# First batch's packed values times w_in: pieces three to eight as three bursts of 512 columns instead of six of 256

## The chip, the cores and the metric

The kernel runs on one core of one Trainium2 chip. The metric is the device time of one execution in microseconds (us); the median of three runs of the kernel before is 786.12 us (785.88 to 786.27). The engines are named as in the profile: PE (TensorE) with its weight loads (PEld), DVE (VectorE), ACT (ScalarE), POOL (GpSimd) and SP (SyncE, which issues the DMAs here).

## The reference

Two attentions, each over 8 batches and 8 heads of width 64, then a feed-forward layer with a rational activation:

```
p_packed = sm_attn(p, k, v)              # 32 packed queries against 576 keys
out      = sm_attn(q, p_packed, p_packed)  # 576 queries against 32 packed keys
x  = out as (4608, 512)
h  = x @ w_in                            # 512 -> 2048
P  = a0 + a1*h + a2*h^2 + a3*h^3
Q  = 1 + |b0|*|h| + |b1|*h^2
out = (P / (Q + 1e-6)) @ w_out           # 2048 -> 512
```

All of it in float32; w_in and w_out arrive as float64 and are taken as their 64-bit words.

## The kernel before, in words

For each batch the kernel never forms `x`. It multiplies the packed values by w_in first (`m`, called M in the code: 2 groups of 128 rows, 2048 columns) and then the softmax weights of the second attention (`AH`) by that: h = m times AH. The 2048 columns of w_in are eight pieces of 256 (`NCH` = 8, `CF` = 256); `m_chunk(bb, c, n)` at lines 786 to 809 makes n of them for batch `bb`, from piece c on. One call is a burst of eight PE products of 64x32 weights into two PSUM tiles of the ring `at` (two buffers of 512 float32 columns), one for each head group, and then, for the first batch, one ACT copy from each PSUM tile into `m`; later batches split into a high and a low part. The ring `at` also serves the attention of all later batches, and the remainder rows.

The feed-forward work is 128 units (batch, half of the 576 rows, piece c). `hidden` (line 814) is one: two tiles `h`, and for each three ACT passes (`Y`, `U`, `sq`) and two DVE passes (`Y` times h, then the step with `abS`), one POOL addition (`U` plus `sq`), two ACT passes (`V`), and two or three DVE passes that end in `gh` or `gl`, the left operand of the last product. `acc_block` (line 893) multiplies it by w_out, three units later, into `acc`. The first 12 units are not divided into a high and a low part; there `gh` belongs to even and `gl` to odd pieces. In the answers of the trace and in the orders below a name such as `h_17` is the 17th tile of that ring: `h_1` and `h_2` are unit 0, `h_17` and `h_18` unit 8; `gh_1`, `gl_1`, `gh_2`, ... are units 0, 1, 2, ...

The float64 words of w_in and w_out come in sixteen pieces, taken into float32 by `convert` (line 429): two ACT passes and three DVE passes (one of them the group that the profile calls CUSTOM_DVE_ANT_0 and the order ISA). In the order below `w_6`, `w_4`, `w_8` are the raw words of w_in's pieces 5, 6 and 7 (counted from one), `w_7`, `w_5`, `w_12`, `w_13` those of w_out.

The text of the kernel does not set the order of issue. Every operation is recorded (all of them appear as line 226 in the profile, the zero products below as line 223) and `Planner` (lines 32 to 231) orders them by a list schedule: costs per engine from a table, priority by the longest way to the end, four rounds, first in, first out on each engine. A buffer ring's turns follow the recorded order, so what is recorded when does matter. The loop at lines 966 to 985 records two halves of each unit u; at each half step `filler(i)` records the burst that `mt` names for step i, and those of the 16 stages of the next batch's attention that `fill` puts there. These stages are spread over the steps of a range that `mt` does not use (line 951). Where the planner's own schedule leaves PE idle early on, `idle` (line 992) adds products with a zero operand into an open accumulation, which change no value.

Of the kernel before, what the change touches and what calls it, by code (L numbers as in the profile page):

```python
# [257 lines left out]
def attention_rational_ffn(  # L258
# [23 lines left out]
    NCH = DF // CF  # L282
# [655 lines left out]

    STEPS = 16
    mt, fill, rem = {}, {}, {}  # L940
    for c in range(1, NCH):
        mt[max(0, 2 * c - 3)] = 0, c
    for bb in range(1, B):
        for c in range(0, NCH, 2):
            mt[2 * UB * bb + 2 * c - 7] = bb, c, 2
# [95 lines left out]
```

## Time and profile before

| | before |
|---|---|
| median of three runs | 786.12 us |
| profiled execution, its time | 788.12 us |
| profiled execution, its span | 786.0 us |
| PE busy | 745.8 us (95%) |
| DVE busy | 693.2 us (88%) |
| ACT busy | 657.8 us (84%) |
| POOL busy | 453.6 us (58%) |
| TensorE clock granted, mean | 0.987 |

A stage table gives the busy time of each engine in a stretch of the span; a chain of waits gives the work that ended last, step by step, with what released it; a row of the timeline gives start, duration, engine and operation, and in brackets the idle time before it and what ended that. Names are out<-in by the program's names, without buffer numbers. The busy time of PE is partly modelled: a row of products that waits inside its run shows as longer.

### The profile page before, as it was taken

The page shows a single profiled execution, that of the slowest core. Times are in us where ns is not written, and L with a number is a line of the kernel's source. Part 1 is how long each engine was busy: PE and PEld are TensorE (multiplying, and loading weights), DVE is VectorE, ACT ScalarE, POOL GpSimd, SP SyncE. Part 2 cuts the span into 40 slices and gives each one's busy share as a digit, 9 for nine tenths or more (in the row PEclk, how much of TensorE's full clock was granted, in tenths as well). Part 3 has the DMA queues.
Part 4 walks back from the last instruction along what each step waited for, and adds up shares of the span by engine and source line. Part 5 has one row for each costly group of instructions (what it writes and reads, how often), then busy time and mean ns, then how long its engine had stood idle before and what let it go on. Part 6 is the DMA issues. An engine that isn't in the chain of part 4 may idle for free.

```text
span 786.0 us, 14945 instructions
## 1 busy us (share of the span) xinstructions
PE 745.8 (95%) x5336; PEld 567.5 (72%) x5336; DVE 693.2 (88%) x1295; ACT 657.8 (84%) x1464; POOL 453.6 (58%) x448
## 2 busy tenths in 40 slices
PE   2679999999999999999999999999999999999997
PEld 1345555588778887678778887678787887778886
DVE  4899999998999789998999789998999789988873
ACT  5869978988896998888897898889798788998872
POOL 0012448757585665756686555756587556766663
PEclk9959999999999999999999999999999999999999
DMA  9984353023601155023601136023701132000001
GB/s 297 332 296 143 108 100 49 1 85 46 110 1 55 45 66 90 1 85 46 95 17 55 44 52 104 1 58 62 94 28 54 41 45 46 1 22 7 27 1 41
DMA packets 152027, 56.03 MB, mean 71 GB/s; under 512 B 122256, under 2 KB 141200, under 8 KB 151952
## 3 DMA queue, kind: packets, MB, share of 16 engines
q1 hardware_dynamic: 151952, 55.07, 30.7%
q8 instruction: 42, 0.69, 0.4%
q14 instruction: 33, 0.27, 0.1%
HBM read 45.62 MB, written 9.44 MB: 70 GB/s over the span
## 4 chain that ended last, share of the span: by engine, by line
PE 76%; ACT 10%; DVE 8%; DMA 4%; issue 1%; POOL 0%; SPq 0%; DVEq 0%; ACTq 0%
PE acc L226 38%; PE h L226 24%; PE at L226 14%; DVE Y L226 4%; ACT Y L226 2%; DMA nat<-in_k_dram 2%; DVE w L226 2%; ACT V L226 1%; ACT U L226 1%; ACT sq L226 1%; ACT kx L226 1%; ACT w L226 1%; DMA m<-in_moe_w_in_dram 1%; ACT m L226 1%; DVE small L226 1%
## 5 line engine op out<-in xcount | busy, mean ns | idle before, releaser
L226 POOL TENSOR_TENSOR U<-U,sq 128x576 f32<-128x576 f32 x128 | 184.1, 1438 | 109.1 <-ACT U L226 55.8
L226 PE MATMUL acc<-w,gh 128*128 128x512 f32 x736 | 239.3, 408 | 1.6 <-ACT gh L226 1.4
L226 PE MATMUL h<-AH,m 128*128 128x288 f32 x1024 | 201.1, 320 | 7.9 <-DVE Y L226 5.6
L226 PEld LDWEIGHTS h<-AH,m 128*128 128x128 f32 x1024 | 163.0, 191 | 45.8 <-DVE Y L226 22.6
L226 POOL TENSOR_TENSOR gl<-Y,gh 128x512 fp32r<-128x512 f32 x116 | 150.2, 1295 | 39.0 <-issue 14.3
L226 PEld LDWEIGHTS acc<-w,gh 128*128 128x128 f32 x736 | 131.8, 188 | 45.5 <-issue 11.8
L226 PE MATMUL acc<-w,gl 128*128 128x512 f32 x384 | 147.9, 412 | 0.0
L226 ACT ACTIVATE Y<-h,abS 128x288 f32<-128x288 f32 x256 | 126.3, 511 | 23.2 <-PE h L226 19.7
L226 ACT ACTIVATE sq<-h 128x288 f32<-128x288 f32 x256 | 107.0, 419 | 39.2 <-PE h L226 31.0
L226 DVE TENSOR_TENSOR Y<-Y,h 128x288 f32<-128x288 f32 x256 | 109.1, 444 | 26.3 <-ACT Y L226 9.7
L226 DVE SCALAR_TENSOR_TENSOR Y<-Y,abS,h 128x288 f32<-128x288 f32 x256 | 124.5, 504 | 2.2
L226 DVE SCALAR_TENSOR_TENSOR Y<-Y,abS,V 128x576 f32<-128x576 f32 x128 | 102.8, 803 | 23.6 <-ACT V L226 23.0
L226 ACT ACTIVATE U<-h 128x288 f32<-128x288 f32 x256 | 98.6, 424 | 9.8 <-PE h L226 4.7
L226 ACT ACTIVATE V<-U,one 128x576 f32<-128x576 f32 x128 | 98.4, 769 | 5.6 <-DVE Y L226 3.8
L226 PE MATMUL h<-AL,m 128*128 128x288 f32 x448 | 96.1, 295 | 0.0
L226 DVE SCALAR_TENSOR_TENSOR V<-U,V 128x576 f32<-128x576 f32 x128 | 96.0, 750 | 0.0
L226 PEld LDWEIGHTS acc<-w,gl 128*128 128x128 f32 x384 | 71.9, 188 | 23.9 <-issue 9.6
L226 DVE SCALAR_TENSOR_TENSOR Y<-V,Y 128x576 f32<-128x576 f32 x116 | 86.7, 748 | 1.9
L226 POOL COPY G<-Y 128x64 f32<-128x64 f32 x116 | 27.5, 237 | 102.6 <-DVE Y L226 95.6
L226 ACT ACTIVATE V<-V 128x576 f32<-128x576 f32 x128 | 84.8, 663 | 0.7
L226 PE MATMUL acc<-half,gh 128*128 128x512 f32 x240 | 78.4, 413 | 1.3 <-ACT gh L226 0.9
L226 ACT CAST gh<-Y 128x512 fp32r<-128x512 f32 x116 | 73.4, 632 | 6.0 <-DVE Y L226 5.5
(135 smaller groups left out, 984.1 us busy)
## 6 DMA issues: line engine op xcount, KB each, us to landing
w<-in_moe_w_out_dram SPq DMA_DIRECT2D x16, 512.0 KB, 4.6
out_dram<-half SPq DMA_DIRECT2D x15, 512.0 KB, 3.1
nat<-in_k_dram SPq DMA_DIRECT2D x48, 144.0 KB, 3.9
nat<-in_q_dram SPq DMA_DIRECT2D x48, 144.0 KB, 4.3
nat<-in_v_dram SPq DMA_DIRECT2D x24, 256.0 KB, 3.7
m<-in_moe_w_in_dram SPq DMA_DIRECT2D x8, 512.0 KB, 6.2
w<-in_moe_w_in_dram SPq DMA_DIRECT2D x8, 512.0 KB, 8.2
nat<-in_k_dram SPq DMA_DIRECT2D x4, 512.0 KB, 7.7
```

Of the source, the lines that this page charges most:

```text
L226: getattr(getattr(self.nc, engine), name)(*args, **kwargs)
```

## The change

The first batch's table of bursts is written otherwise. Piece 1 (counted from zero) stays at step 0; pieces 2 and 3 are now one call at step 1, pieces 4 and 5 one at step 5, pieces 6 and 7 one at step 9. Before, pieces 2 to 7 stood singly at steps 1, 3, 5, 7, 9 and 11. Pieces 3, 5 and 7 are thus recorded two steps earlier, and need their piece of w_in converted by then.

```diff
     STEPS = 16
     mt, fill, rem = {}, {}, {}
-    for c in range(1, NCH):
-        mt[max(0, 2 * c - 3)] = 0, c
+    mt[0] = 0, 1
+    for c in range(2, NCH, 2):
+        mt[2 * c - 3] = 0, c, 2
     for bb in range(1, B):
         for c in range(0, NCH, 2):
             mt[2 * UB * bb + 2 * c - 7] = bb, c, 2
```

Since `mt` no longer names steps 3, 7 and 11, line 951 has three more steps to spread the second batch's attention over: its 16 stages stood at steps 2, 4, 6, 8, 12, 13, 14, 15, 17, 18, 19, 20, 22, 23, 24, 26 and now stand at 2, 3, 4, 7, 8, 11, 12, 14, 15, 16, 18, 19, 21, 22, 24, 26.

The planner then orders everything anew. On every engine the order is the same again, row for row, from the third batch's first units on (on PE from the 618th of 2567 rows; the tile `h_64`, the end of the second batch). The difference lies before that. Three places follow.

The first place is ACT's queue behind the conversion of w_in's sixth piece (`w_4`). `at_18` to `at_22` are tiles of the ring `at`; the copies into `kx` carry the second batch's transposed keys. Before:

```order
L226 ACTIVATE win<-w_4_118 128x1024
L226 COPY kx_2_142<-at_18_144 128x512
L226 COPY kx_2_142<-at_19_145 128x512
L226 ACTIVATE U_1_125<-h_1_129 128x288
L226 ACTIVATE sq_1_128<-h_1_129 128x288
L226 ACTIVATE U_1_125<-h_2_132 128x288
L226 ACTIVATE sq_1_128<-h_2_132 128x288
L226 ACTIVATE Y_1_127<-h_1_129,abS 128x288
L226 ACTIVATE Y_1_127<-h_2_132,abS 128x288
L226 COPY m_6_134<-at_20_149 128x256
L226 COPY m_6_134<-at_21_150 128x256
L226 ACTIVATE w_5_119<-w_5_119 128x1024
```

And now, at the same place of ACT's queue:

```order
L226 ACTIVATE win<-w_4_118 128x1024
L226 COPY kx_2_142<-at_18_144 128x512
L226 ACTIVATE w_5_119<-w_5_119 128x1024
L226 ACTIVATE Y_1_127<-h_1_129,abS 128x288
L226 ACTIVATE U_1_125<-h_1_129 128x288
L226 ACTIVATE sq_1_128<-h_1_129 128x288
L226 ACTIVATE U_1_125<-h_2_132 128x288
L226 ACTIVATE sq_1_128<-h_2_132 128x288
L226 ACTIVATE w_10_159<-w_5_119 128x1024
L226 COPY kx_2_142<-at_19_145 128x512
L226 ACTIVATE Y_1_127<-h_2_132,abS 128x288
L226 COPY kx_2_142<-at_20_149 128x512
```

The two passes over `w_5` (a piece of w_out that a DMA brings) moved ahead of unit 0's activations, and the copy of `at_19` moved behind them.

The second place is DVE's queue around `gh_4` (unit 6). Before:

```order
L226 TENSOR_SCALAR small<-at_41_231,small 128x128
L226 SCALAR_TENSOR_TENSOR V_7_207<-U_7_206,V_7_207 128x2x288
L226 SCALAR_TENSOR_TENSOR small<-at_41_231,small 128x128
L226 SCALAR_TENSOR_TENSOR gh_4_235<-V_7_207,Y_7_208 128x512
L226 SCALAR_TENSOR_TENSOR G<-V_7_207,Y_7_208 128x2x32
L226 TENSOR_TENSOR Y_9_228<-Y_9_228,h_17_230 128x288
L226 TENSOR_TENSOR Y_9_228<-Y_9_228,h_18_234 128x288
L226 SCALAR_TENSOR_TENSOR Y_9_228<-Y_9_228,abS,h_17_230 128x288
```

And now:

```order
L226 SCALAR_TENSOR_TENSOR V_7_204<-U_7_203,V_7_204 128x2x288
L226 TENSOR_SCALAR w_15_201<-w_15_201 128x1024
L226 SCALAR_TENSOR_TENSOR gh_4_235<-V_7_204,Y_7_205 128x512
L226 TENSOR_TENSOR Y_9_225<-Y_9_225,h_17_227 128x288
L226 SCALAR_TENSOR_TENSOR G<-V_7_204,Y_7_205 128x2x32
L226 SCALAR_TENSOR_TENSOR Y_9_225<-Y_9_225,abS,h_17_227 128x288
```

Ahead of `gh_4` stand the same operations on DVE in both, in another order. The last row shown frees the buffer in which PE writes `h_19`.

The third place is PE's queue from `gl_3` (unit 5) to `h_19`. Before:

```order
L223 MATMUL acc_14_172<-w_16_215,zero 64x96 x4
L226 MATMUL acc_13_171<-w_16_215,gl_3_225 128x512 x2
L226 MATMUL h_17_230<-AH_3_113,m_5_122 128x288 x2
L226 MATMUL h_18_234<-AH_3_113,m_5_122 128x288 x2
L226 MATMUL at_41_231<-ident,small 128x128
L226 MATMUL acc_14_172<-w_16_215,gl_3_225 128x512 x2
...
L226 MATMUL at_42_237<-ident,nat_7_232 128x128 x3
L226 MATMUL acc_13_171<-w_17_236,gh_4_235 128x512
L226 MATMUL at_43_238<-ident,nat_7_232 128x128 x4
...
L226 MATMUL at_44_240<-ident,AH_2_107 128x128 x4
L226 MATMUL h_19_247<-AH_3_113,m_5_122 128x288 x2
```

And now:

```order
L226 MATMUL h_17_227<-AH_3_113,m_5_122 128x288 x2
L226 MATMUL acc_14_170<-w_16_210,gl_3_222 128x512
L226 MATMUL at_37_229<-ident,nat_7_219 128x128 x4
L226 MATMUL at_38_231<-ident,AH_2_107 128x128 x4
L226 MATMUL h_18_234<-AH_3_113,m_5_122 128x288 x2
...
L226 MATMUL at_39_237<-ident,nat_8_220 128x128 x4
L226 MATMUL at_40_238<-ident,nat_8_220 128x128 x4
L226 MATMUL h_19_244<-AH_3_113,m_5_122 128x288 x2
L226 MATMUL acc_13_169<-w_17_236,gh_4_235 128x512 x2
```

The two products of `gh_4` into `acc_13`, of 512 columns each, moved behind `h_19`, and the eight transposes of `nat_8` moved ahead of it. Everything else ahead of `h_19` is the same work, apart from the bursts and the zero products, of which there are now 20 instead of 12.

## The prediction

> **What bounds the kernel now.** First the stage table of before (us of the stretch, then the busy us of each engine, the granted TensorE clock, the DMA share, GB/s):
>
> ```profile
> span 786.0 us, 14945 instructions
> ...
> 40.00:63.00 23.00, 17.26 (x69) 9.54 (x68) 21.20 (x32) 16.02 (x31) 3.77 (x3) 0.58 0.79 280
> 63.00:110.00 47.00, 45.35 (x322) 24.64 (x321) 45.54 (x82) 42.43 (x88) 18.37 (x13) 1.00 0.37 117
> 110.00:240.00 130.00, 129.79 (x858) 92.96 (x858) 119.58 (x232) 114.87 (x258) 89.20 (x84) 1.00 0.29 50
> 240.00:786.00 546.00, 535.70 (x3828) 428.86 (x3826) 480.24 (x897) 456.16 (x1041) 340.38 (x343) 1.00 0.24 46
> ```
>
> Three stages after the loading of the first 40 us, in which the change has nothing that matters. From 40 to 63 a mixed chain, at a low clock. From 63 to 110 PE, DVE and ACT are all above 90%; DVE has 1.46 us free. From 110 to 240 PE is idle for 0.21 us in all, DVE for 10.4. So whatever the change saves must be there when PE's queue closes up near 110; from then on a us of PE is a us of time. Since the order is the same again behind the second batch, the difference at about 240 is the difference at the end, unless later waits absorb it.
>
> Then the chain of waits, for how the first stage hands over to PE (start, us, what):
>
> ```profile
> 40.00 5.30 DMA w<-in_moe_w_in_dram
> ...
> 47.62 2.96 DVE w L226 x3
> ...
> 53.79 4.22 PE h L226 x8
> ...
> 59.66 1.10 PE at L226 x14
> 60.77 2.21 PE h L226 x4
> ...
> 111.97 0.86 PE acc L226 x2
> 112.83 0.44 PE at L226 x4
> 113.26 0.97 PE h L226 x4
> ```
>
> The words of w_in's sixth piece land at 45.30; two ACT passes later, at 47.62, DVE takes them. Up to there the two orders do the same work on DVE. The first bursts stand in this stage, and all of them end before 110, where PE still waited for others.
>
> **What the change saves by itself: nearly nothing.** Twelve ACT copies of 256 columns become six of 512, six bursts become three. The rows for both sizes (the 512 ones are of later batches; min/median/max ns; for PE, start and us):
>
> ```profile
> L226 ACT COPY m<-at x16: 372/420/673, 35.5 to 85.9; 128x256 f32<-128x256 f32 x16
> L226 ACT CAST m<-at x56: 571/597/694, 139.8 to 690.4; 128x512 fp32r<-128x512 f32 x56
> 84.63 0.66 PE L226 MATMUL at<-win,ppT 64*32 64x256 f32 x16
> 213.19 1.09 PE L226 MATMUL at<-win,ppT 64*32 64x512 f32 x16
> ```
>
> ACT: 12 x 0.420 - 6 x 0.597 = 1.5 us. PE: 6 x 0.66 - 3 x 1.09 = 0.7 us. No DVE row and no byte of DMA goes. Both savings lie before 110, where DVE is the engine without room, so I cost them at nothing: DVE's rows are the cover. If that cover were gone they would be worth at most the 0.7 of PE.
>
> **What the new order moves.** I follow DVE, since the rows ahead of `gh_4` on it are the same set. These are its idle times from 47.62 to there, and `gh_4` itself:
>
> ```profile
> 59.17 0.45 DVE L226 TENSOR_TENSOR Y<-Y,h 128x288 f32<-128x288 f32 x1 [0.44 <-ACT sq L226]
> 64.13 0.45 DVE L226 TENSOR_TENSOR Y<-Y,h 128x288 f32<-128x288 f32 x1 [0.68 <-ACT sq L226]
> 65.12 0.46 DVE L226 TENSOR_TENSOR Y<-Y,h 128x288 f32<-128x288 f32 x1 [0.54 <-ACT sq L226]
> 71.38 0.45 DVE L226 TENSOR_TENSOR Y<-Y,h 128x288 f32<-128x288 f32 x1 [0.20 <-ACT sq L226]
> 109.68 0.67 DVE L226 SCALAR_TENSOR_TENSOR gh<-V,Y 128x512 f32<-128x512 f32 x1
> ```
>
> They sum to 1.86 us, 1.12 of it before 64.13. `gh_4` ends at 110.35. In the new order it ends at 110.35 less the lead that DVE wins or loses; the lead cannot be more than about 1.9 us.
>
> The wait that the change adds: on ACT the two passes over `w_5` now stand ahead of unit 0's activations. Behind them wait unit 0's `Y`, `U`, `sq`, then POOL and DVE, and, since the copy of `at_19` went behind them too, the transposes of `nat_4` on PE and `h_3` behind those. When do the words of `w_5` land?
>
> ```profile
> 44.00:46.00 2.00, 1.83 (x5) 0.86 (x4) 2.00 (x3) 0.61 (x1) 0.00 (x0) 0.50 1.05 303
> 46.00:48.00 2.00, 2.00 (x4) 0.91 (x4) 0.64 (x2) 2.00 (x4) 0.00 (x0) 0.50 0.91 355
> 48.00:50.00 2.00, 1.40 (x17) 0.40 (x16) 2.00 (x3) 2.00 (x8) 0.20 (x1) 0.71 1.03 391
> ...
> w<-in_moe_w_out_dram SPq DMA_DIRECT2D x16, 512.0 KB, 4.6
> 48.40 0.44 ACT L226 ACTIVATE U<-h 128x288 f32<-128x288 f32 x1
> 50.85 1.26 ACT L226 ACTIVATE w<-w 128x1024 f32<-128x1024 f32 x1
> 75.59 0.41 DVE L226 TENSOR_REDUCE small<-at 128x1 f32<-128x256 f32 x1
> 80.50 0.68 DVE L226 TENSOR_SCALAR w<-w 128x1024 int32<-128x1024 int32 x1
> ```
>
> `w_5` is two DMAs of 512 KB; after 45.30 at 303 to 391 GB/s, with 128 KB of another load ahead, they need some 3.3 us: about 48.6 (an estimate). The upper bound is 50.85, where ACT took them in before without waiting. The lower bound is no wait at all, 48.0.
>
> With 48.6 I walk on with the durations of before. ACT: first pass to 49.8, unit 0's five activations to 51.5, second pass to 52.7, copy of `at_19` to 53.2. PE: transposes, then `h_3` at about 53.8, where it also started in before (53.79), because there it waited for DVE, which now takes `w_7`'s last pass first. Then the 512-column burst of pieces five and six, `h_4`, the transposes of `AH_2` and `pn_2`, and `h_5` at 60.3 to 60.9 against 60.77. So unit 2 starts as before, and PE has more behind it, at a time when it had room. On DVE I come to 63.9 with two reductions (0.41 each) done that before did later, and one `w` pass (0.68) less, against 64.13: a lead of 0.23 + 0.82 - 0.68 = 0.4 us. I take 0.3; from 64.13 to 110 I leave the idle time as it was. The bounds: 1.86 above; below, the landing at 50.85, which is 2.25 later, -1.95.
>
> **The sum.** PE's queue closes where it must wait last. In before that was at 109.81 (0.61 us for DVE's `small`); in the new order those `small` rows stand earlier, and the last such place is `h_19`, whose buffer DVE frees three rows behind `gh_4` (0.40 + 0.21 + 0.46 by the rows for these operations at 110.41, 110.27 and 111.13):
>
> ```profile
> 103.34 1.99 PE L226 MATMUL acc<-w,gl 128*128 128x512 f32 x4
> 104.24 0.33 DVE L226 TENSOR_SCALAR small<-at,small 128x128 f32<-128x128 f32 x1
> 109.81 0.33 PE L226 MATMUL at<-ident,small 128*128 128x128 f32 x1 [0.61 <-DVE small L226]
> 110.27 0.21 DVE L226 SCALAR_TENSOR_TENSOR G<-V,Y 128x64 f32<-128x64 f32 x1
> 110.41 0.80 DVE L226 TENSOR_TENSOR Y<-Y,h 128x288 f32<-128x288 f32 x2
> 111.13 0.92 DVE L226 SCALAR_TENSOR_TENSOR Y<-Y,abS,h 128x288 f32<-128x288 f32 x2
> ```
>
> - By DVE `h_19` starts at 110.35 - 0.3 + 1.07, about 111.1, against 113.26.
> - At that point the new order has two products of `gh_4` still to do, which before had done (0.86 each: the row at 111.97): +1.72; and eight transposes done which before had not (0.11 each: the row at 112.83 has four in 0.44): -0.88. Net +0.84.
> - PE itself is there hardly sooner: from `gl_3` it has four products (3.44), `h_17` and `h_18` (0.97 each by the row at 113.26, 1.94) and 19 transposes (2.09), 7.5 us. `gl_3` started at 103.34 in before; on DVE it now has 0.66 more ahead of it (two `small` rows of 0.33), less the lead: 103.7, plus 7.5 is 111.2. I take the later, 111.2.
>
> Sum: 111.2 - 113.26 + 0.84 = **-1.2 us**. Against the profiled execution: 786.0 to 784.8 in span, 788.12 to 786.9 in time. That execution's time is 2.0 above the median; the difference is put on the median: **784.9 us**. The zero products (20 rows for 12) cost nothing in this sum: they stand where PE waits.
>
> **The rivals.** A difference under 0.2% (1.6 us, so 784.5 to 787.7) is what a measurement of this kernel can hardly tell from none.
>
> 1. The clock comes up earlier: 783.3. In before the clock fell to half where PE idled, and stayed there:
>
> ```profile
> 52.00:54.00 2.00, 0.21 (x1) 0.21 (x2) 2.00 (x4) 2.00 (x4) 0.00 (x0) 0.64 0.16 50
> 54.00:56.00 2.00, 2.00 (x5) 1.43 (x6) 2.00 (x4) 1.86 (x3) 0.00 (x0) 0.50 1.10 413
> 58.00:60.00 2.00, 1.32 (x9) 0.33 (x16) 1.56 (x5) 1.97 (x5) 0.79 (x1) 0.50 1.00 391
> 62.00:64.00 2.00, 2.00 (x10) 1.45 (x9) 1.45 (x2) 1.14 (x5) 0.00 (x0) 0.80 0.03 8
> ```
>
> From 53.8 on the new order gives PE more to do without a gap (burst and transposes where before waited at 58.0 to 59.66). If the clock is full from 59, `h_4` and `h_5` each take 0.97 instead of 2.21 or so, and DVE's waits for them, 0.68 + 0.54 + 0.44, go: 784.9 - 1.6. Against it: four busy us from 54 did not raise it in before. The Trainium skill, page TensorE: Matmul & The Clock Gate, section Part 1: The HAM clock gate, says that the array runs at half rate until one window of about 3.4 us was busy. By that rule a PE busy without a gap from 53.8 is at full rate by 60.6 at the latest, which is this rival. The trace neither bears it out nor denies it: PE was busy from 54 to 58, but the clock came back only between 62 and 64, after the gap of 58 to 60.
>
> 2. Nothing is left: 786.1. The reordered units are late on DVE (ahead of `gh_3` it now takes both conversions of one w_out pair, 3.8 us more), PE waits there, and what it did ahead only fills that wait. For it: the planner put 14 of the 20 zero products between `gh_2` and `gh_3`. Against it: the set ahead of `gh_4` is equal.
>
> 3. Slower: 787.8. ACT's queue stands at `w_5`. From a landing at 49.5 on, every us of it is a us of unit 0, because copy, transposes and `h_3` are all behind. At 50.85 unit 0 is 2.25 later, which turns -1.2 into +1.0; PE then idles through 49.8 to 56, and the half clock lasts over `h_5` and `h_6`, 2 x 0.6 us more, part of it on the path: +1.7. For it: nothing in the trace shows the landing itself. Against it: the DMA rates.
>
> 4. That the change does not do what it says: the order shows three bursts of 512, so no; that the planner scatters the rest of the kernel is excluded by the equal rows.
>
> **How the numbers follow.** Forecast 0.43 (784.9, its own range 784.2 to 785.9), the clock 0.22, nothing left 0.15, slower 0.20. Faster by over 0.2%: nearly all of the clock, 0.21, and the lower third of the forecast, 0.15, together 0.36. Slower by over 0.2%: rival 3 but for its milder end, 0.17. Between: 0.47. The range takes in the clock case with a lead of 1.9 and the slower case's centre: 782.8 to 787.8.
>
> **What would show it.** Right: in the new trace ACT's first pass over `w_5` starts near 48.6; `h_3` near 53.8; `gh_4` on DVE ends at 109.5 to 110.4; `h_19` starts near 111; PE idles less than 0.5 us from there to 240; the copies of 512 columns take about 0.6. Rival 1: clock at 1.00 before 62 and `gh_4` before 109.2. Rival 3: an ACT idle time of over 1 us ahead of `w_5` that ends by its DMA, and `gh_4` after 111.5. The forecast is wrong if PE shows waits for DVE between 112 and 240, or if the lead is lost again in the later batches, where DVE and ACT end 5 us of PE's waits.

## The result, and the profile after

| | before | the change |
|---|---|---|
| median | 786.12 us (785.88 to 786.27) | 791.05 us (788.87 to 792.55, four executions) |
| ratio | | 1.0053, 95% interval 1.0036 to 1.0071 |
| profiled execution, time and span | 788.12, 786.0 us | 788.87, 786.8 us |

The change makes the kernel slower, by 4.9 us here, and by 2.5 and 4.1 us where it was timed again later (r1 and r10 below). The forecast was 784.9, and the range ended at 787.8.

The stage table of the change (us of the stretch, then busy us of PE, PEld, DVE, ACT and POOL, granted TensorE clock, DMA share, GB/s), and the group of the new copies:

```profile
span 786.8 us, 14882 instructions
...
40.00:63.00 23.00, 17.84 (x101) 9.76 (x87) 21.56 (x35) 17.81 (x35) 3.91 (x3) 0.70 0.88 300
63.00:110.00 47.00, 45.30 (x284) 25.55 (x284) 46.09 (x82) 42.25 (x84) 17.87 (x13) 1.00 0.35 111
110.00:240.00 130.00, 127.38 (x843) 91.29 (x842) 121.21 (x230) 112.63 (x254) 88.59 (x85) 1.00 0.31 49
...
L226 ACT COPY m<-at 128x512 f32<-128x512 f32 x6 | 3.4, 636 | 1.2 <-PE at L226 1.2
```

The six copies are there (636 ns each). From 110 to 240 PE was busy for 129.79 us in before and is now busy for 127.38: it stands idle for 2.62 us instead of 0.21. That is the stage in which a us of PE is a us of time.

`h_19`, where the prediction lets PE's queue close up, did come earlier, as forecast. These are the rows of the change's timeline for it (PE's `h_3`; DVE's `gh_4`; PE's `h_19`):

```profile
53.34 0.92 PE L226 MATMUL h<-AH,m 128*128 128x288 f32 x2
...
109.04 0.68 DVE L226 SCALAR_TENSOR_TENSOR gh<-V,Y 128x512 f32<-128x512 f32 x1
...
110.81 1.14 PE L226 MATMUL h<-AH,m 128*128 128x288 f32 x4
```

In before the same rows stood so: DVE's two steps that free the buffers of `h_19` and `h_20`, PE's `h_19`, the row of `w_15` on DVE, PE's `h_20`, and PE's only wait between 110 and 240:

```profile
111.13 0.92 DVE L226 SCALAR_TENSOR_TENSOR Y<-Y,abS,h 128x288 f32<-128x288 f32 x2
...
113.10 1.14 PE L226 MATMUL h<-AH,m 128*128 128x288 f32 x4
...
114.04 1.21 DVE L226 CUSTOM_DVE_ANT_0 w<-w,w 128x2048 uint16<-128x2048 uint16 x1
...
114.95 1.14 PE L226 MATMUL h<-AH,m 128*128 128x288 f32 x4
...
223.15 0.73 PE L226 MATMUL acc<-w,gh 128*128 128x512 f32 x2 [0.21 <-ACT gh L226]
```

`h_19` starts 2.29 us earlier than the 113.10 of before. (The 113.26 of the chain of waits is the end of the row ahead of it, which overlaps.) Then come waits that before did not have. The waits of PE over 1 us behind 63, and one of the smaller ones, of the change:

```profile
97.00 1.55 PE L226 MATMUL acc<-w,gh 128*128 128x512 f32 x3 [1.42 <-DVE gh L226]
...
115.69 1.24 PE L226 MATMUL h<-AH,m 128*128 128x288 f32 x4 [1.16 <-DVE Y L226]
...
135.87 1.24 PE L226 MATMUL h<-AH,m 128*128 128x288 f32 x4 [0.28 <-DVE Y L226]
...
222.89 0.50 PE L226 MATMUL acc<-w,gh 128*128 128x512 f32 x1 [1.18 <-ACT gh L226]
```

For the two profiled executions this closes. PE starts the same burst of the later batches at 257.69 in before and at 258.49 in the change. From `h_19` to there it is busy for 144.38 and 145.06 us: -2.29 us at `h_19`, +0.68 us of work that was done ahead of `h_19` in before and is now behind it, +2.41 us of PE waits (2.62 against 0.21). That is +0.80, and the spans differ by 0.8.

Where PE's queue closes up is best read from the chain of waits. In before the chain passes from DVE to PE at 109.81 and stays there for the next 100 us. In the change it stays on DVE and ACT for 26 us longer, up to 135.87. Its pieces behind 42 us that matter here, and that place:

```profile
42.30 5.58 DMA w<-in_moe_w_out_dram
...
48.51 1.17 ACT w L226
...
135.30 0.53 DVE Y L226
135.83 0.04 issue
135.87 1.24 PE h L226 x4
```

**Why the two medians lie further apart than that.** The kernel before was profiled twice more (r11 and r12 below), the change too (r1, r10). The start of `gh_4` on DVE stands for all that comes ahead of it:

| profiled execution | `gh_4` starts | span | from there to the end |
|---|---|---|---|
| before | 109.68, 108.57, 107.33 | 786.0, 785.0, 783.8 | 676.3, 676.4, 676.5 |
| the change | 109.04, 111.09, 109.92 | 786.8, 789.0, 787.8 | 677.8, 677.9, 677.9 |

Behind `gh_4` the two kernels never overlap: the change needs 1.44 us more by the means, and 1.3 to 1.6 in every pairing. Ahead of it each kernel scatters by about 2 us; by the means the change is 1.5 us later there, which three against three do not settle. The profiled execution of before was the slowest of its three and that of the change the quickest. Over all timed executions the medians of the spans are 784.7 for before (115 executions on five chips, 783.1 to 787.4; only 17 of them at 786.0 or above) and 787.9 for the change (17 executions, 786.2 to 790.4): 3.2 us apart. With 1.44 us of that behind `gh_4`, some 1.8 us lie ahead of it (an estimate): more than half of what a typical execution loses. Part of it is seen on DVE, which from 40 us to `gh_4` waits for ACT for 2.15, 2.75 and 2.08 us in the three profiles of the change, and for 1.15 and 1.26 us in r11 and r12 (3.22 in the first profile of before, the slowest).

### The profile page after: what moved, and what is told of

Read it like the earlier page. It is cut to its first block, busy times and chain, and to the rows that moved or that the text cites. A ratio compares the mean times of both kernels' runs of the same rounds, so it can differ in the third digit from the quotient of the medians.

```text
span 786.8 us, 14882 instructions
## 1 busy us (share of the span) xinstructions
PE 746.5 (95%) x5304; PEld 569.1 (72%) x5304; DVE 695.5 (88%) x1295; ACT 657.4 (84%) x1458; POOL 452.9 (58%) x448
## 4 chain that ended last, share of the span: by engine, by line
PE 73%; DVE 11%; ACT 10%; DMA 4%; issue 1%; SPq 1%; POOL 0%; DVEq 0%; ACTq 0%
PE acc L226 36%; PE h L226 23%; PE at L226 14%; DVE Y L226 5%; DMA nat<-in_k_dram 2%; ACT Y L226 2%; DVE w L226 2%; ACT U L226 1%; ACT sq L226 1%; ACT V L226 1%; DVE small L226 1%; DVE V L226 1%; DMA AH<-in_k_dram 1%; ACT w L226 1%; ACT m L226 1%
## 5 line engine op out<-in xcount | busy, mean ns | idle before, releaser
L226 PEld LDWEIGHTS h<-AH,m 128*128 128x128 f32 x1024 | 161.2, 189 | 45.0 <-DVE Y L226 24.1
L226 DVE TENSOR_TENSOR Y<-Y,h 128x288 f32<-128x288 f32 x256 | 109.8, 445 | 26.8 <-ACT Y L226 9.4
```

The lines of the kernel that those rows point to most:

```text
L226: getattr(getattr(self.nc, engine), name)(*args, **kwargs)
```

## The experiments

Ratios are to the kernel before, run on the same chip at the same time (its medians there: 786.48 to 787.4 us). The last three columns are of the run's own profile. PE idle is the sum of the waits of 0.15 us and more ahead of the PE rows that start between 63 and 262 us. "PE closes" is the start of the PE row at which the chain of waits last passes to PE ahead of 200 us; in before the two are 1.9 and 109.81, in the change's first profile 4.3 and 135.87.

| run | kernel | median us | ratio, 95% interval | `gh_4` starts | PE idle | PE closes |
|---|---|---|---|---|---|---|
| r1 | the change again | 789.85 | 1.0037, 1.0020 to 1.0054 | 111.09 | 5.1 | 137.93 |
| r2 | merged, attention steps of before | 787.88 | 1.0005, 0.9994 to 1.0016 | 107.90 | 2.5 | 117.44 |
| r3 | six bursts, attention on the freed steps too | 788.54 | 1.0018, 1.0008 to 1.0028 | 110.13 | 4.2 | 143.30 |
| r4 | steps of the change, two bursts of 256 each | 787.69 | 1.0007, 0.9997 to 1.0017 | 110.14 | 3.7 | 103.33 |
| r5 | change, `w_5`'s first pass behind unit 0 | 789.49 | 1.0028, 1.0015 to 1.0040 | 109.54 | 4.3 | 136.38 |
| r6 | change, two PE waits mended | 790.74 | 1.0043, 1.0030 to 1.0055 | 108.74 | 3.4 | 136.46 |
| r7 | r5 and r6 together | 789.95 | 1.0037, 1.0025 to 1.0049 | 108.80 | 3.4 | 136.54 |
| r8 | before, `w_5`'s first pass ahead of unit 0 | 788.16 | 1.0008, 0.9998 to 1.0018 | 109.20 | 2.1 | 109.33 |
| r9 | change, all rows of `w_5` late | 794.83 | 1.0097, 1.0083 to 1.0111 | 114.85 | 8.6 | 141.68 |
| r10 | the change again | 790.62 | 1.0052, 1.0040 to 1.0065 | 109.92 | 4.3 | 136.76 |
| r11, r12 | before, one profile each | 787.14, 785.92 | | 108.57, 107.33 | 1.9, 1.5 | 108.70, 107.47 |
| r13 | merged, attention later (first way) | 788.19 | 1.0015, 1.0006 to 1.0024 | 111.17 | 5.1 | 175.94 |
| r14 | merged, attention later (second way) | 788.37 | 1.0029, 1.0019 to 1.0039 | 107.70 | 2.7 | 173.31 |
| r15 | change, DVE behind `gh_4` in the order of before | 790.32 | 1.0044, 1.0030 to 1.0059 | 110.31 | 3.9 | 138.68 |
| r16 | r4, one PE wait mended | 787.38 | 1.0007, 0.9999 to 1.0016 | 111.20 | 2.6 | 104.40 |
| r17 | before, pieces 2 and 3 merged only | 790.63 | 1.0048, 1.0034 to 1.0062 | 109.10 | 7.4 | 135.61 |
| r18 | before, pieces 6 and 7 merged only | 788.16 | 1.0012, 1.0001 to 1.0024 | 107.62 | 2.7 | 146.47 |

**First: which part of the change does it?** The change has three parts that can be done apart: bursts of 512, pieces recorded earlier, and the second batch's attention on the freed steps 3, 7 and 11.

r1, the change as it is:

> The changed kernel once more, for how far its single executions lie apart. Theory A (the new order has fixed waits: 1.16 us at the product h_20 near 115, 1.18 at 222.9): executions within 0.5 us of each other, near 788 to 789, as the profile of the changed kernel has it (span 786.8). Theory B (the new order sits on an edge: which instruction comes first on some engine depends on when a DMA lands or on the phase of something free-running): executions spread over 3 us or more again, 788 to 793, while the kernel before keeps within 0.5 us; then the profile shown was a lucky one.

r2, merged, but the attention may not use the freed steps, so that it stands where it stood in before:

```diff
-        at = [... if u not in mt]
+        at = [... if u not in mt and u not in (3, 7, 11)]
```

> Three bursts of 512 columns as in the change, but the second batch's attention stages stay at the steps they had before. Theory C (the moved attention stages cost the time): as fast as before or up to 1 us faster, 785 to 786.5, and close together. Theory D (the merged bursts cost it): about 791, as far apart as the change.

r3, the six bursts of before, but the attention may use steps 3, 7 and 11 as well:

```diff
-        at = [... if u not in mt]
+        at = [... if u not in mt or u in (3, 7, 11)]
```

> Six bursts of 256 columns at their old steps, only the second batch's attention stages at the steps that the change gives them. Theory C: about 791, and spread. Theory D: 786, close together. If both this and the one with merged bursts alone are slow, any new order of the planner's is, and the old one was a good draw.

r4, the change's steps, but each merged call made as two bursts of 256:

```diff
-            m_chunk(*mt[i])
+            m_chunk(0, c)
+            m_chunk(0, c + 1)
```

> Pieces as early as in the change and attention stages at the change's steps, but two bursts of 256 columns at each of the three places instead of one of 512. If the width of the bursts matters by itself: 0.7 us of PE and 1.5 us of ACT more than the change, up to 2 us slower. If only the order matters: anywhere between 785 and 793, since the planner orders it anew.

Measured: 1.0037, 1.0005, 1.0018, 1.0007. The loss is there again when the change is run again, and none of the three kernels with less than all parts has the whole of it. Merged bursts, which bring their pieces forward, cost nothing that can be told where the attention stays (r2); early pieces with the change's attention steps cost nothing that can be told where they are bursts of 256 (r4); the attention's steps alone cost a third to a half of it (r3). r2 is the merge that this change could have been, and it is no faster than before either. Neither theory of r1 holds as written: the change's seven executions lie 3.8 us apart, but the thirty of before beside them lie 3.5 apart.

**Second: the rows that the prediction rests on, moved by hand.** In these kernels the planner's order is kept and single operations, with what depends on them, are issued directly behind another one, by a list of pairs. The numbers below are those of operations in the recorded order.

r5, ACT's first pass over `w_5` behind unit 0's five activations:

```diff
+HAND = [(311, 228)]
```

> The change with one row moved on ScalarE: the first pass over w_5 stands behind unit 0's five activations instead of ahead of them; nothing else differs. The change measured 2.4 us over the kernel before on one chip. Theory W (ScalarE's queue stands at w_5 until that piece has landed, and unit 0 is late by that much up to the end of the kernel): unit 0's first activation starts at about 48.5 instead of 49.6 to 51.0, the gain is 1.0 to 2.5 us, so 0 to 1.4 us over the kernel before; PE's two waits of 1.2 us (at h_20 and at 222.9) stay. Theory N (the start has slack, and only the two later waits and chance cost the time): 2.4 us over before, as the change.

r6, two waits of PE mended: DVE takes the step with `abS` of `h_18`, for which `h_20` waits, one row earlier; and PE's product of `gh_21`, for which it waited at 222.89, goes behind five remainder products:

```diff
+HAND = [(593, 592), (1565, 1599)]
```

> The change with w_5 left ahead of unit 0 and the two later waits mended: on DVE h_18's last step goes ahead of unit 8's 576-column step (0.73 us earlier), and on PE one product of gh_21 goes behind five remainder products that were ready. Both theories give PE's wait at h_20 as about 0.4 instead of 1.16 us and the one at 222.9 as under 0.2 instead of 1.18. If what is gained there reaches the end: 1.7 us faster than the change, so about 0.7 us over the kernel before. If later work is waiting for something else and takes the gain back: 2.4 us over, as the change.

r7, both:

```diff
+HAND = [(311, 228), (593, 592), (1565, 1599)]
```

> The change with all three moves: w_5's first pass behind unit 0, h_18's step earlier on DVE, the product of gh_21 later on PE. Theory W: both gains add, 2.7 to 4.2 us faster than the change, so 0.3 to 1.8 us faster than the kernel before (ratio 0.998 to 1.000). Theory N: 1.7 us faster than the change, 0.7 us over the kernel before (ratio 1.001).

r8, the other way round: the kernel before, with `w_5`'s first pass ahead of unit 0:

```diff
+HAND = [(314, 258)]
```

> The kernel before, its six bursts and steps kept, with one row moved on ScalarE: the first pass over w_5 stands ahead of unit 0's activations, as it does in the change. Theory W: unit 0's first activation starts at about 49.6 to 51 instead of 48.4, and the kernel becomes 1.0 to 2.5 us slower (ratio 1.001 to 1.003). Theory N: within 0.3 us of the kernel before.

Measured: 1.0028, 1.0043, 1.0037, 1.0008. Nothing came back that can be told from r1 and r10, though a gain of about 1 us could hide in intervals of this width. Where the rows went can be seen in three timelines: PE in r5, ACT and DVE in r8, and PE in r7.

```profile
52.66 0.87 PE L226 MATMUL at<-ident,nat 128*128 128x128 f32 x4 [3.45 <-ACT kx L226]
```

```profile
49.43 1.21 ACT L226 ACTIVATE w<-w 128x1024 f32<-128x1024 f32 x1 [0.58 <-issue]
50.47 0.46 ACT L226 ACTIVATE U<-h 128x288 f32<-128x288 f32 x1
...
109.20 0.67 DVE L226 SCALAR_TENSOR_TENSOR gh<-V,Y 128x512 f32<-128x512 f32 x1
```

```profile
114.86 1.24 PE L226 MATMUL h<-AH,m 128*128 128x288 f32 x4 [0.57 <-DVE Y L226]
...
136.54 1.24 PE L226 MATMUL h<-AH,m 128*128 128x288 f32 x4 [0.38 <-DVE Y L226]
```

In r5 PE still waits 3.45 us for the copy of `at_19`, which still stands behind `w_5`. In r8 unit 0 starts 2 us later than in before (50.47 against 48.40), and `gh_4` nevertheless starts at 109.20, between the three values of before. So that profile shows no loss; the twelve timed executions lie 1.1 us above before's median, with an interval of -0.2 to 1.4 us, between what the two theories said. In r7 the wait for `h_20` is halved, and the wait near 136 grows from 0.28 to 0.38. From `gh_4` to the end r6 needs 678.0 us and r7 678.5, no less than the 677.8 to 677.9 of the change. The last column of the table fits that: the chain leaves DVE only at 136.5, no sooner behind `gh_4` than in the change.

**Third: `w_5` as a dose, and the kernels again.** r9, the change with all five conversion rows of `w_5` late: the ACT passes behind unit 0's second `V` and behind the copy of `at_23`, DVE's first row behind the step with `abS` of `h_3`, its other two behind `gh_1`:

```diff
+HAND = [(311, 269), (312, 320), (313, 248), (314, 305)]
```

> The change with all five rows of w_5 moved back to where the kernel before has them: ScalarE's two passes behind unit 0's V step and behind the copies of at_22 and at_23, VectorE's three rows behind h_3's step and behind gh_1. In the run that moved ScalarE's first pass alone, the copy of at_19 and all that follows it still stood behind w_5. Theory W (the landing of w_5, which scatters, delays the start of the change): unit 0, at_19 to at_23 and h_3 no longer wait for it; gh_4 starts near 108 instead of 109.0 to 111.1, and the time falls by 1 to 1.5 us against the change on the same chip, with a spread of some 3 us instead of 4 to 5. Theory D (VectorE's queue beyond gh_4 holds attention rows of the second batch earlier than before, and that alone costs the time): within 0.4 us of the change on the same chip, because those rows stay.

> The change itself, on the chip of the run with w_5 late, as its measure. Every theory: 2.0 to 3.5 us over the kernel before, as on the two other chips; from gh_4 to the end 677.8 us, as in its two profiles so far, against 676.3 in the kernel before.

> The kernel before, for a second profile: its first one, with a span of 786.0 us, was among the slowest of its 52 spans, whose median is 785.0. Theory D: from gh_4 to the end 676.3 us again, so that the rest, about 1 us less, is found ahead of gh_4. If the part behind gh_4 is shorter instead, the fixed difference to the change is larger than 1.5 us.

> The kernel before, for a third profile, with the same question: gh_4 at about 108.5 to 109.7 and 676.3 us from there to the end.

Measured: r9 is much slower, 1.0097, and PE's timeline of r9 says why:

```profile
66.65 1.22 PE L226 MATMUL acc<-w,gh 128*128 128x512 f32 x1 [2.19 <-DVE w L226]
```

The first product of the feed-forward needs the words of `w_5`. In this order they cannot go as late as in before. So r9 does not give the price of `w_5` ahead of unit 0: it replaces one wait by a longer one. r11 and r12 gave the table of three against three above; r12's `gh_4`, at 107.33, came sooner than the 108.5 to 109.7 expected.

**Fourth: the attention's steps as a dose.** First a correction. The section on the change above lists the steps of the second batch's 16 stages wrongly. They stand at 2, 4, 6, 8, 12, 13, 14, 16, 17, 18, 20, 21, 22, 24, 26, 27 in before and at 2, 3, 6, 7, 10, 11, 13, 14, 16, 17, 19, 20, 22, 23, 26, 27 in the change. No term of the sum used them.

In the change DVE has 48 attention rows ahead of `gh_3` and 56 ahead of `gh_5`, in before 43 and 52; 36 of them are the first batch's in every kernel, the others the second batch's. If these others are what makes DVE late, fewer of them should make it quicker. r13 has 39 and 52 rows, r14 has 36 and 52; both have the three merged bursts.

```diff
-        at = [... if u not in mt]
+        at = [... if u not in mt and u not in (2, 3, 4, 7, 11)]      # r13
+        at = [... if u not in mt and u not in (2, 3, 4, 6, 7, 8)]    # r14
```

> The three bursts of 512 columns kept, the second batch's attention stages moved later: their first steps are 6, 8, 10, 12 instead of 2, 3, 6, 7 (2, 4, 6, 8 in the kernel before). VectorE's queue then has 39 attention rows ahead of gh_3 instead of 48 (43 before) and 55 ahead of gl_5 instead of 61 (55 before). Theory D (each attention row ahead of PE's next product costs its half us while VectorE sets the pace): at least as fast as merged bursts at the old steps (1.0005), so a ratio of 0.997 to 1.000. Rival T (the later attention rows only move the wait to the second batch, whose bursts need them): 1.001 or more, with PE waits between 140 and 240.

> The same with a larger dose: first steps 10 to 17 without a gap; 36 attention rows ahead of gh_3, 53 ahead of gl_5. ScalarE's first pass over w_5 stands ahead of unit 0 in this order, as in the change. Theory D: faster again or the same as the smaller dose, 0.995 to 1.000. Rival T: slower than the smaller dose. If w_5's place mattered by itself, slower than the smaller dose by 1 us or more already at gh_1.

r15, the change with DVE's rows behind `gh_4` as before has them (`h_18`'s two rows ahead of `w_15`'s conversion, the last row of that conversion behind `Y`), and the product of `gh_21` moved as in r6:

```diff
+HAND = [(593, 592), (648, 593), (649, 599), (1565, 1599)]
```

> The change with VectorE's order behind gh_4 as in the kernel before (both steps of h_18, then w_15's row, unit 8's step, and the joining of w_15 last of these), and PE's product of gh_21 behind the remainder products. The joining of w_15 then starts near 113.3 us, clear of GpSimd's addition (111.4 to 113.0), and should take 1.2 us instead of 2.3; PE's wait of 1.16 us at h_20 should be gone whole. If stretched rows and waits there are what costs: 1.5 to 2 us faster than the change, 1.000 to 1.003. If the attention rows in VectorE's queue set the pace up to 137 us anyway: 0 to 0.8 us faster than the change, 1.003 to 1.005.

r16, r4 with the product of `gh_21` moved:

```diff
+HAND = [(1574, 1608)]
```

> The pieces and attention stages of the change, but two bursts of 256 columns for each pair (which measured 1.0007 of the kernel before), with PE's product of gh_21 behind the five remainder products that were ready, as its one wait over 0.5 us beyond 110 us stood there (1.18 us at 221.4). If that wait reaches the end: 1 us faster, ratio 0.9990 to 1.0000. If it is taken back at the next wait, as it seemed with all three moves: 1.0007 again.

Measured: 1.0015 and 1.0029 for fewer rows, against 1.0005 for r2 with 44: there is no dose. So the number of attention rows by itself does not set the time. Rival T's sign came, PE waits between 140 and 240 that before does not have, but small ones (0.37 us at 175.94 in r13, 0.45 at 173.31 in r14). r16, with its wait mended, stays at 1.0007 as r4. r15 is the plainest test of the wait at `h_20`. In the change DVE stood so behind `gh_4`:

```profile
110.56 1.21 DVE L226 SCALAR_TENSOR_TENSOR w<-w 128x1024 int32<-128x1024 int32 x1
111.80 2.32 DVE L226 CUSTOM_DVE_ANT_0 w<-w,w 128x2048 uint16<-128x2048 uint16 x1
...
115.14 0.50 DVE L226 SCALAR_TENSOR_TENSOR Y<-Y,abS,h 128x288 f32<-128x288 f32 x1
```

The last row frees the buffer of `h_20`; 3.5 us of `w_15`'s conversion stand ahead of it. DVE and PE in r15:

```profile
113.11 0.52 DVE L226 SCALAR_TENSOR_TENSOR Y<-Y,abS,h 128x288 f32<-128x288 f32 x1
...
115.63 1.13 PE L226 MATMUL h<-AH,m 128*128 128x288 f32 x4
115.81 1.21 DVE L226 CUSTOM_DVE_ANT_0 w<-w,w 128x2048 uint16<-128x2048 uint16 x1
...
118.47 1.12 PE L226 MATMUL acc<-w,gl 128*128 128x512 f32 x2 [0.21 <-DVE gl L226]
120.44 1.24 PE L226 MATMUL h<-AH,m 128*128 128x288 f32 x4 [0.84 <-DVE Y L226]
```

`h_20` no longer waits. But 5 us later PE stands for 0.21 and 0.84 us at DVE's `gl` and `Y`, and further waits of up to 0.37 us follow to 139. From `gh_4` to the end r15 needs 678.8 us, 0.9 more than the change, and the time stays at 1.0044. In the change DVE, with 28.83 us of work in the 30 us from 110 to 140, has no slack in which a row could go:

```profile
110.00:140.00 30.00, 28.55 (x132) 14.94 (x131) 28.83 (x58) 25.42 (x54) 22.35 (x19) 1.00 0.39 51
```

The same stretch of before (r11):

```profile
110.00:140.00 30.00, 30.00 (x141) 16.31 (x140) 28.05 (x59) 26.74 (x57) 19.92 (x16) 1.00 0.40 58
```

**Fifth: one pair at a time.** The kernel before, with one merged call only, that of pieces 2 and 3 (counted from zero) in r17 and that of pieces 6 and 7 in r18; every other piece stands singly.

```diff
-    for c in range(1, NCH):
-        mt[max(0, 2 * c - 3)] = 0, c
+    for c in (1, 2, 4, 5, 6, 7):                                      # r17
+        mt[max(0, 2 * c - 3)] = (0, c, 2) if c == 2 else (0, c)
+    for c in (1, 2, 3, 4, 5, 6):                                      # r18
+        mt[max(0, 2 * c - 3)] = (0, c, 2) if c == 6 else (0, c)
```

> The kernel before with only the third and fourth piece in one burst of 512 (at step 1); the others keep their bursts of 256 and steps, and one attention step (3) comes free. On ScalarE w_5 stays behind unit 0. If the loss is the early burst in front of unit 0's successors: 1.002 to 1.005. If it belongs to the order as a whole, with all three merged: 1.000 to 1.0015.

> The kernel before with only the seventh and eighth piece in one burst of 512 (at step 9); step 11 comes free for attention. If the loss is the attention rows moved up by a freed step: 1.001 to 1.003, with PE idle between 110 and 140 us as in the change (1.4 us). If the late pair is free, as merged bursts at the old attention steps were: 0.9990 to 1.0010.

Measured: r17, 1.0048, is as slow as the whole change; r18, 1.0012, has about a quarter to a third of it. Each also frees a step of the attention (3 and 11), so neither is the merge alone. The waits of PE in r17:

```profile
63.21 1.13 PE L226 MATMUL acc<-w,gh 128*128 128x512 f32 x2 [2.24 <-DVE w L226]
...
78.56 1.24 PE L226 MATMUL h<-AH,m 128*128 128x288 f32 x4 [1.10 <-DVE Y L226]
...
135.61 1.24 PE L226 MATMUL h<-AH,m 128*128 128x288 f32 x4 [1.08 <-DVE Y L226]
...
223.96 0.50 PE L226 MATMUL acc<-w,gh 128*128 128x512 f32 x1 [1.18 <-ACT gh L226]
```

They are at other places than in the change (at 135.61 where the change has 115.69), and of the same kind: PE in its queue, DVE's row for it behind other DVE rows.

**What the runs settle, and what they leave open.** Settled: none of the parts run by itself or with one other has the whole loss (r2, r3, r4). The first pair and the attention step that it frees are enough to have all of it (r17), and all three pairs are free when the attention stands otherwise (r2). So the cost belongs to the whole order that the planner makes of a set of steps: on DVE, which is over 90% busy from 40 to 240, it puts rows that PE waits for behind rows that PE does not wait for. That such waits stand behind `gh_4` is shown (+2.41 us from 110 to 240 for the profiled pair), and so is that mending them one by one does not give the time back (r6, r7, r15).

Neither `w_5`'s place (r5, r8; 1.4 us at most by r8's interval), nor the count of attention rows (r13, r14), nor PE's summed waits (r4 with 3.7 us loses nothing that can be told, r6 and r7 with 3.4 lose as much as the change) foretell a run's time. The last column of the table parts them: before and the four kernels that cannot be told from it (r2, r4, r8, r16) hand the chain to PE by 118 us, and every kernel that is slower clear of noise does so at 135 or later. It was read off the profiles afterwards, one profile per run, and it does not give the size of a loss (r17 closes at 135.61 and loses four times what r18 loses, at 146.47); so it is a sign and not yet a shown cause. Open as well: what delays `gh_4` in a typical execution of the change. No version beat the kernel before: the best, r2, r4 and r16, cannot be told from it.

## Why the prediction was wrong, point by point

The forecast lies 6.15 us below the median. That is the sum's own error of 1.95 (a gain of 1.2 forecast, a loss of 0.75 in the time of the profiled pair), the 2.0 that was put on the median, and 2.18 by which the change's profiled execution lies below its own median.

- *Burst and copies at nothing.* Right: r2 has all six wide copies and three wide bursts, and shows no gain.
- *Landing of `w_5`.* ACT's first pass started at 48.51, forecast 48.6. In r1 it started at 49.92; these are the rows of the change and of r1:

```profile
48.51 1.17 ACT L226 ACTIVATE w<-w 128x1024 f32<-128x1024 f32 x1 [0.63 <-issue]
```

```profile
49.92 1.15 ACT L226 ACTIVATE w<-w 128x1024 f32<-128x1024 f32 x1 [1.33 <-DMA w<-in_moe_w_out_dram]
```

- The second is rival 3's stand of ACT's queue, longer than in the profiled pair. In all three profiles of the change the chain of waits goes back over the landing of `w_5` (47.88, 49.85 and 48.71), where in the three of before it goes back over that of w_in's sixth piece; so this wait is on the path ahead of `gh_4`. Its price is not settled: `w_5`'s first pass ahead of unit 0 has `gh_4` at 109.8 (mean of five profiles), behind it at 109.2 (two).
- *A lead of 0.3 on DVE; `h_3` at 53.8, `gh_4` done at 109.5 to 110.4, `h_19` at 111.1 to 111.2.* Measured 53.34, 109.72 and 110.81. Right for that execution, and partly by luck: in r1 `gh_4` ends at 111.77, and by the means of three against three the lead is a loss of 1.5 us. The forecast took one row of a scattered quantity as a fixed one: ahead of `gh_4` the three profiles of before spread over 2.35 us, more than any term of the sum.
- *+0.84 us of work left.* Near: 0.68 by the busy times of the pair.
- *The last place where PE must wait is `h_19`, and from there to 240 PE idles under 0.5 us.* **The step that failed.** PE's queue closed at 135.87, and PE idled for 2.62 us. The working followed DVE only to the row that frees `h_19`, and took for granted that behind it DVE would be ahead, as in before, where the buffer of `h_20` was free 2.9 us ahead of PE (112.05 against 114.95). In the change the row for `h_20` stands at 115.14 behind two rows of `w_15`. That the lead goes could be read from the order: with the later row at the 1.21 us that it takes in before, DVE would be done near 114.5, just where PE comes free. That row took 2.32 us, beside a POOL addition (last section), and the 1.11 us more are nearly the whole wait of 1.16; no duration in the prediction held that. The 1.18 us at 222.89 are the order's: in before five products of the remainder stand ahead of that row that now stand behind it. The text named "waits for DVE between 112 and 240" as what would make it wrong, but gave them no price.
- *"The difference is put on the median".* **Also failed.** The saving was counted against an execution that was among the slowest 15% of its kernel, then subtracted from the median. What that execution lost by itself (a clock of 0.50 from 54 to 62 and of 0.80 from 62 to 64, DVE waiting for 3.22 us from 40 to `gh_4` where r11 and r12 have 1.15 and 1.26) is not there to be saved in a typical one.
- *Rival 1, the clock earlier.* Half of its sign came: full clock from 58; but `gh_4` ended at 109.72, not before 109.2. And r11 and r12 of before have the full clock from 58 too, so it is no gain over a typical execution. Rows of the change, then of r12:

```profile
54.00:56.00 2.00, 2.00 (x11) 0.56 (x17) 2.00 (x4) 1.60 (x5) 0.00 (x0) 0.50 0.97 363
56.00:58.00 2.00, 1.89 (x19) 0.67 (x4) 2.00 (x4) 1.70 (x5) 0.00 (x0) 0.75 0.91 299
58.00:60.00 2.00, 2.00 (x12) 1.37 (x11) 2.00 (x4) 2.00 (x5) 0.00 (x0) 1.00 1.05 402
```

```profile
56.00:58.00 2.00, 1.42 (x5) 0.39 (x3) 1.87 (x4) 1.39 (x6) 0.00 (x0) 0.87 1.00 397
58.00:60.00 2.00, 1.45 (x18) 0.89 (x19) 1.95 (x4) 2.00 (x6) 1.42 (x1) 1.00 0.82 330
```

- PE has no wait of 0.15 us or more from 52.84 to 60 in the change, and the clock is full at about 57 (0.50 from 54 to 56, 0.75 from 56 to 58), some 4 us later. The Trainium skill, page TensorE: Matmul & The Clock Gate, section Part 1: The HAM clock gate, has the array at full rate once one window of about 3.4 us was busy; this trace agrees. The first profile of before, busy from 53.79 to 58.98 at a clock of 0.50, does not bear it out.
- *Rival 2, nothing left.* Its mechanism came, PE waiting 1.42 us for `gh_3` at 97.00 (in before its longest wait there was 0.70, at 96.39); its time, 786.1, did not. It was given 0.15.
- *Rival 3, slower.* The right side, 3.2 us short of the median. Its sign came whole in r1 (ACT idle for 1.33 us up to the DMA, `gh_4` done at 111.77), so its mechanism may be part of what is lost ahead of `gh_4`; the 1.44 us behind `gh_4` are another.

## What to carry to other kernels

Where a list schedule orders the work, an edit of a few steps is a new draw of the whole order, and its own saving (here 2.2 us of engine time, all hidden) says little about the result; follow the engine without slack row by row to the place where the chain of waits leaves it for good, not to the first place where its consumer seems served. Profile the kernel before more than once: count savings against the execution that gave the rows, but only those that a median execution has to give. Where an engine is 96% busy and the chain runs over it, a single mended wait of its consumer moves on to the next (r6, r7, r15); what helped here was another order as a whole (r2, r4).

## What the runs showed of the hardware

**DVE rows stretched beside POOL's.** Two DVE rows of the change took eight times and nearly twice the time of the same operation elsewhere, with a POOL operation under way. DVE's row and POOL's in the timeline of the change:

```profile
88.00 3.54 POOL L226 TENSOR_TENSOR half<-w,half 128x512 fp32r<-128x512 f32 x2 [0.59 <-ACT half L226]
...
88.58 1.22 DVE L226 SCALAR_TENSOR_TENSOR small<-small 128x2 f32<-128x2 f32 x1
...
111.39 1.64 POOL L226 TENSOR_TENSOR U<-U,sq 128x576 f32<-128x576 f32 x1 [1.14 <-DMA nat<-in_k_dram]
```

And the two-column row in before (r11):

```profile
96.25 0.15 DVE L226 SCALAR_TENSOR_TENSOR small<-small 128x2 f32<-128x2 f32 x1
```

The two-column row took 1.22 us under POOL's addition and 0.15 elsewhere; the conversion row at 111.80 took 2.32 us, and 1.21 in r15. The 2.32 row began at 111.80 and ended at 114.12, behind POOL's row that ended at 113.03. Rows stretched by over 0.25 us add up to 4.2 us from 45 to `gh_4` in before and 3.5 to 3.8 in the change; from `gh_4` to 140 to 0.25 at most in before and 1.4 in the change, in all three profiles of each. That these 1.4 us make the 1.44 us behind `gh_4` is not shown: in r15 that row was short again and the time did not change.

The Trainium skill, page SBUF — State Buffer, section SBUF: two separate sides, says that DVE and GpSimd share a port pair, which is locked for a whole instruction while the loser blocks. The rows agree with it; they do not show which forms of operation are free of it.

**Time outside the span.** An execution takes 2.09 to 2.22 us beyond its span in all 115 of before. In the change it takes over 2.5, up to 3.26, in 5 of 17, and so do some of r5, r6, r7 and r9, four of the five kernels made from the change by hand, and none of r15, the fifth, nor of any other run. In r3 it is 1.74 to 1.86 in all twelve. It is part of why the medians of the time lie further apart than those of the span. Its cause was not looked into.
